# Four transposed loads a chunk instead of sixteen, and half the pause between a chunk's last load and its logits, in a convolution and mixture-of-experts kernel

## The chip, the cores and the metric

The kernel runs on one core of a Trainium2 chip. The metric is the device time of one execution in microseconds. The engines are TensorE (PE, matmuls; PEld its weight loads), VectorE (DVE), ScalarE (ACT), GpSimd (POOL) and SyncE (SP), which issues most of the DMAs.

## The reference

Eight sequences of 3,584 tokens with 192 features pass a causal convolution of 7 taps whose softmaxed weights differ by head; its 28,672 output tokens pass a mixture of 8 experts, one expert a token.

```python
# convolution: 8 heads of 24 features, softmax over the 7 taps
out = np.einsum('hk,bskhg->bshg', w, x_unf)          # (8, 3584, 192)
# routing and experts, x is out as (28672, 192)
xn = x / (norm(x) + 1e-6);  en = emb / (norm(emb) + 1e-6)
logits = xn @ en.T / tau
expert_idx = argmax(logits, axis=1)
probs = softmax(logits)                              # gate = probs[expert_idx]
for e in range(8):
    mask = expert_idx == e
    h = np.maximum(x[mask] @ w1[e], 0.0)             # (n, 1024)
    out[mask] = gate_w[mask, None] * (h @ w2[e])     # (n, 192)
```

## The kernel before

The tokens are cut into 16 chunks of 1,792: 16 tiles of 112 tokens (`TP`), token on the partition. A chunk passes these stages.

- `mix`: for each head one band matmul (L389) convolves all 16 tiles; ACT copies the result out (L392); ACT or DVE sums the squares.
- `route`: in four groups of four tiles (`GX`), `scaled` (L436, L438) and `rest` (L445 on) write each token as fp16 high and low parts into its row in `rows2`. A row has `RW` = 240 words of 4 bytes: 448 fp16 values, then the token's number and gate. `turn` (L624) transposes the rows' first 384 columns, so that features lie on the partitions: one DMA on SP's queue for each tile, written to a slot of `xtb`. After the last of them the stage pauses by `TURN`; then `logits` (L612) does three small matmuls a tile, and `rank` takes the argmax, the gate and each token's place (`pc`, `di`). Chunks 0 and 1 are transposed on TensorE, in the head; chunks 2 to 15 by these DMAs.
- `put`, `scatter` (L628): POOL writes each tile's rows by indirect DMA into `rows_d` in DRAM, sorted by expert.
- `hand_out`, after chunks 2, 3, 5, 8 and 12 (`PICK`), and `last_blocks` at the end: `select` (L663 to L712), some 20 tiny DVE instructions on one partition, chooses the expert and first row of blocks of 1,024, 512, 256 and at the end 128 tokens (`sel`). At the end nine scatters of zero rows (`pads`) come first.
- An expert block: `fetch` on SP reads the first row from `sel` (L745), loads the block's rows transposed (`e_xT`, two DMAs, L753) and the tokens' numbers and gates (`e_mt`, L757). For each of 8 steps five matmuls give the hidden values in PSUM (`h_ps`, L799), ACT takes the relu (L803), DVE the low part (L805). Then for each 128 tokens 24 matmuls (`o_ps`, L822), ACT scales them by the gate into `y` (L827, a ring of four buffers), and POOL writes them out by token number (`out_dram`, L829). Five PSUM banks serve `h_ps` and `o_ps` in turn.

The order is made when the kernel is built. The expert steps carry a clock (about 1.07 us for a step of first products and 1.92 for 128 tokens of second ones); a dispatcher puts the pieces of `mix` and `route` between them, and a pause such as `TURN` holds the next piece until the clock has moved on by that much. DMAs on SP stand in its program in the order in which they were written, and SP takes them one after another; a scheduler orders the other engines.

Of the kernel before, what the change touches and what calls it, by code (L numbers as in the profile page):

```python
# [12 lines left out]
F16 = mybir.dt.float16  # L13
# [12 lines left out]
D = 192  # L26
E = 8
# [4 lines left out]
CT = TP * NT  # L32
XD = 224
RW = 240


W2 = 3 * F
# [5 lines left out]
NFC = F // 128  # L43
PICK = (2, 3, 5, 8, 12)
GX = 4
XW = GX * 3 * TP
NACT = 3
PRE = 39
TURN, RANK, GAP = 14.0, 10.0, 0.5
STEP = 5 * 512 / 2400, 24 * D / 2400  # L50
RAW = 2 * (2 * F + F * D // 128)
AREAS = (1, 0), (1, 2), (1, 1), (0, 0), (0, 1), (1, 0), (0, 0), (0, 1)
# [23 lines left out]
class _Moe:  # L76
    def __init__(self, ctx, tc, x, weight, emb, tau, w1, w2, out):
        self.tc, self.nc = tc, tc.nc
        self.x, self.weight, self.emb, self.tau = x, weight, emb, tau
        self.w1, self.w2, self.out = w1, w2, out  # L80
        B, S, _ = x.shape
        self.B, self.S, self.N = B, S, B * S
        self.nch = self.N // CT
        self.per_b = S // CT
        self.cap = self.N + PAD
        self.dummy = E * self.cap
        pool = lambda name, bufs, **k: ctx.enter_context(
            tc.tile_pool(name=name, bufs=bufs, **k))
        self.cp = pool("const", 1)
        self.xp = pool("xload", 2)  # L90
        self.sp = pool("small", 2)
        self.lp = pool("lone", 1)
        self.ep = pool("expert", 3)
        self.yp = pool("y", 3)
        self.op = pool("out", 4)
        self.mp = pool("meta", 6)
        self.rings = {k: pool("ps_" + k, n, space=PSUM)
                      for k, n in (("r", 2), ("l", 1), ("h", 5))}

        self.res = self.cp.tile([128, E * RES], F16, name="res")  # L100
        self.work = self.cp.tile([128, 2 * NFC * 512 + S2 + RES - W2], F16, name="work")
        self.hid = self.work[:, 0:2 * NFC * 512]
        self.slot = self.work[:, 2 * NFC * 512:]
        self.xtb = self.cp.tile([128, NT // GX, XW + HALO], F16, name="xtb")
        self.rows2 = self.cp.tile([TP, 2, NT, RW], I32, name="rows2")
        self.ids = self.cp.tile([TP, NT], I32, name="ids")
        self.xtn = 0
        self.wexp = self.cp.tile([128, E, 2], I32, name="wexp")
        self.dp = pool("scratch", 1, space=DRAM)
        self.rows_d = self.dp.tile([E * self.cap + PAD, RW], I32, name="rows_d")  # L110
        self.scatters, self.pend, self.step = [], [], None
        self.nput, self.final = 0, False
        self.counts, self.pace = {}, 1.0
        self.xts, self.mixed = [], {}
        self.subs, self.ready, self.at, self.copied = [], 0, 0, 0
        self.clock, self.mm = 0.0, None
# [50 lines left out]

    def constants(self):
        nc, cp = self.nc, self.cp
        nc.gpsimd.memset(self.xtb[:, :, XW:], 0.0)  # L170
        nc.gpsimd.memset(self.rows2[:, :, :, XD + 2:], 0)
        nc.gpsimd.iota(self.ids, pattern=[[TP, NT]], base=TP - 1,
                       channel_multiplier=-1)
        head = self.ep.tile([128, 4 * 512], F16, tag="xT", name="head")[:].bitcast(F32)
        self.idf, self.onef = head[:, 0:128], head[:, 128:256]
        make_identity(nc, self.idf)
        self.idh = cp.tile([128, 128], F16, name="idh")
        nc.vector.tensor_copy(out=self.idh, in_=self.idf)
        nc.gpsimd.memset(self.onef, 1.0)
        self.oneh = cp.tile([128, 128], F16, name="oneh")  # L180
        nc.gpsimd.memset(self.oneh, 1.0)

        self.lth = cp.tile([128, 128], F16, name="lth")
        nc.gpsimd.memset(self.lth, 1.0)
        nc.gpsimd.affine_select(
            out=self.lth, in_=self.lth, pattern=[[1, 128]], base=0,
            channel_multiplier=-1, compare_op=ALU.is_gt, fill=0.0)

        tmp = self.op.tile([128, D], F32, tag="y", name="tmp")[:, 0:2 * E + 64].bitcast(I32)
        e8i = tmp[0:TP, 0:E]  # L190
        nc.gpsimd.iota(e8i, pattern=[[-1, E]], base=E, channel_multiplier=0)
        self.e8 = cp.tile([TP, E], F32, name="e8")
        nc.vector.tensor_copy(out=self.e8, in_=e8i)

        self.rst = cp.tile([TP, E, NT], F32, name="rst")
        nc.gpsimd.memset(self.rst, 1.0)
        nc.gpsimd.memset(self.rst[:, :, 0:1], 0.0)

        nums = tmp[0:1, E:E + 64]
        nc.gpsimd.iota(nums, pattern=[[1, 64]], base=0, channel_multiplier=0)  # L200
        self.nums = cp.tile([1, 64], F32, name="nums")
        nc.vector.tensor_copy(out=self.nums, in_=nums)

        cbi = tmp[:, E + 64:]
        nc.gpsimd.iota(cbi, pattern=[[self.cap, E]], base=0, channel_multiplier=0)
        self.cb = cp.tile([128, E], F32, name="cb")
        nc.vector.tensor_copy(out=self.cb, in_=cbi)

        self.start = cp.tile([1, E], F32, name="start")
        nc.vector.tensor_copy(out=self.start, in_=cbi[0:1, :])  # L210
# [231 lines left out]
    def rest(self, c, g):  # L442
# [5 lines left out]
        self.nc.vector.tensor_tensor(  # L448
            out=rows[:, u, 320:384], in0=xc[:, u, 128:192],
            in1=rows[:, u, 256:320], op=ALU.subtract)  # L450
        self.nc.vector.tensor_copy(out=rows[:, u, 384:448], in_=rows[:, u, 256:320])


    def route(self, c):
# [23 lines left out]
    def first(self, c):  # L478
# [9 lines left out]
        for v in steps:  # L488
# [4 lines left out]
            else:  # L493
# [4 lines left out]
                for a in range(GX):  # L498
# [2 lines left out]
                        in_=rows[:, g * GX + a, k * 128:(k + 1) * 128],  # L501
                        identity=self.idh[:TP, :TP])
                nc.scalar.copy(  # L503
                    out=xT[:, 0:XW].rearrange("p (a k t) -> p a k t", k=3, t=TP)[:, :, k, :],
                    in_=tp)
                if k == 2:
                    if g == 0:
# [6 lines left out]
    def rank(self, c, lg, f):  # L514
# [63 lines left out]
        di = sp.tile([TP, NT], I32, tag="di", name="di")  # L578
        nc.vector.tensor_single_scalar(out=di, in_=dr, scalar=-1.0, op=ALU.add)
        yield 0.8, 0.0  # L580
        self.pend += [(c, di[:, t:t + 1], r32[:, t, :]) for t in range(NT)]
        self.left += CT
        if c + 1 in PICK[1:]:
            self.hand_out(c + 1)
# [23 lines left out]
    def logits(self, lg, xT, g):  # L608
        for a in range(GX):
            for k in range(3):  # L610
                u = (a * 3 + k) * TP
                i = self.nc.tensor.matmul(  # L612
                    out=lg[:, g * GX + a, :], lhsT=xT[:, u:u + 128],
                    rhs=self.mb if k == 2 else self.ma,
                    start=(k == 0), stop=(k == 2))
                if k == 0:
                    self.behind(i)


    def turn(self, c, g):  # L620
        xT, rows, t = self.xt_next(), self.rows2[:, c % 2].bitcast(F16), g * GX
        xv = xT[:, 0:XW].rearrange("p (a k t) -> p a k t", k=3, t=TP)
        for a in range(GX):
            self.nc.sync.dma_start_transpose(out=xv[:, a], in_=rows[:, t + a, 0:2 * D])  # L624
        return xT

    def scatter(self, idx, src):
# [29 lines left out]
    def select(self, n, k, last, name, cb):  # L657
# [17 lines left out]
        nc.vector.scalar_tensor_tensor(out=bs, in0=ap, scalar=-float(n),  # L675
                                       in1=self.start, op0=ALU.mult, op1=ALU.add)
        jf = self.nums[:, 0:k]
        ge, df = one("ge", (1, k, E + 1), F16), one("df", (1, k, E))
        nc.vector.memset(ge, 1.0)
        nc.vector.tensor_tensor(  # L680
            out=ge[:, :, 1:], in0=a[:].unsqueeze(1).to_broadcast([1, k, E]),
# [3 lines left out]
        nc.vector.tensor_tensor(  # L685
            out=df, in0=df, in1=bs[:].unsqueeze(1).to_broadcast([1, k, E]),
            op=ALU.mult)
        ro, tm, se = one("ro", (1, k)), one("tm", (1, k)), one("se", (1, k))
        nc.vector.tensor_reduce(out=ro, in_=df, op=ALU.add, axis=AX.X)
        nc.vector.scalar_tensor_tensor(out=ro, in0=jf, scalar=float(n), in1=ro,  # L690
                                       op0=ALU.mult, op1=ALU.add)
# [353 lines left out]
```

## Time and profile before

| | us |
|---|---|
| three runs | 1232.15, 1233.92, 1236.98 |
| median | 1233.92 |
| the profiled execution | 1238.18 |
| its span | 1236.5 |
| TensorE busy | 1127.5 (91%) |
| DVE / ACT / POOL busy | 756.1 / 587.4 / 550.4 |

The span lies 1.7 us inside the profiled execution's time, and that execution 4.3 us above the median. A page of the profile gives the busy time of each engine, the span in 40 slices (about 31 us each), and groups of instructions by their line. In its last columns "<-" names what ended the idle time ahead of an instruction. The head, in which weights are loaded and chunks 0 and 1 are routed, takes until about 113 us; from there to about 842 us routing runs between expert blocks; after that there are expert blocks alone.

### The profile page before, as it was taken

To read this page: it belongs to the slowest core of one execution; us is meant where nothing else is said; L and a number is where in the kernel's file an instruction comes from. 1 tells how busy PE (TensorE), PEld (TensorE's weight loads), DVE (VectorE), ACT (ScalarE), POOL (GpSimd) and SP (SyncE) were. 2 spreads that over 40 slices of the span, in tenths; PEclk is the share of its full clock that TensorE was granted. 3 is DMA by queue.
4 is the path that set the end of the run, shared out by engine and by line. 5 is a ranking of instruction groups with operands and counts; after the bars stand their busy time and mean duration, and the time that the engine had idled before them with its cause. 6 is when DMAs were issued, how large, how long until landed. Compare 5 with 4: busy or idle time off the path is not lost.

```text
span 1236.5 us, 31375 instructions
## 1 busy us (share of the span) xinstructions
PE 1127.5 (91%) x10428; PEld 872.4 (71%) x10428; DVE 756.1 (61%) x2029; ACT 587.4 (48%) x1350; POOL 550.4 (45%) x522
## 2 busy tenths in 40 slices
PE   4675769899999899998989999999999999999998
PEld 2553658786677876756877676666677777898897
DVE  2899766886668757666675746553434453466365
ACT  4986445554554555563635454423333333333333
POOL 0074165574575645565745546673222222222222
PEclk9676879899999999999989999999999999999999
DMA  9945566576675576755638545326122231123121
GB/s 243 231 131 157 119 157 150 126 164 122 150 173 146 109 158 134 161 144 107 164 73 191 110 86 134 90 87 107 43 54 49 52 72 49 44 48 71 43 57 43
DMA packets 305818, 140.68 MB, mean 114 GB/s; under 512 B 247630, under 2 KB 296141, under 8 KB 305664
## 3 DMA queue, kind: packets, MB, share of 16 engines
q1 hardware_dynamic: 282000, 87.97, 34.3%
q0 software_dynamic: 23664, 50.68, 14.5%
q8 instruction: 94, 1.54, 0.5%
q14 instruction: 60, 0.49, 0.1%
HBM read 38.35 MB, written 51.05 MB: 72 GB/s over the span
## 4 chain that ended last, share of the span: by engine, by line
PE 37%; issue 8%; POOL 3%; DMA 3%; ACT 1%; DVE 1%; POOLq 0%; ACTq 0%; DVEq 0%
PE h_ps L799 18%; PE o_ps L822 17%; POOL out_dram L829 2%; POOL rows_d L628 1%; PE conv_ps L389 1%; DMA rows_d<-rows,di 1%; DMA xtb<-rows 1%; DMA out_dram<-y,e_mt 1%; ACT work L803 1%; DVE work L805 0%; DMA rows_d<-xtb,padi 0%; ACT rows L438 0%; ACT sq L402 0%; PE lg_ps L612 0%; DVE work L735 0%
## 5 line engine op out<-in xcount | busy, mean ns | idle before, releaser
L822 PE MATMUL o_ps<-work 128*128 128x192 f16 x5472 | 497.8, 248 | 21.3 <-DVE work L805 9.9
L822 PEld LDWEIGHTS <-work 128*128 128x128 f16 x5472 | 458.5, 99 | 59.9 <-DVE work L805 15.9
L829 POOL DMA_INDIRECT out_dram<-y,e_mt x228 | 255.1, 1119 | 470.8 <-ACT y L827 434.0
L805 DVE SCALAR_TENSOR_TENSOR work<-h_ps,work 128x512 f16<-128x512 f32 x456 | 311.1, 687 | 169.0 <-ACT work L803 165.2
L803 ACT ACTIVATE work<-h_ps 128x512 f16<-128x512 f32 x456 | 267.5, 596 | 236.5 <-PE h_ps L799 205.5
L628 POOL DMA_INDIRECT rows_d<-rows,di x256 | 281.6, 1100 | 141.4 <-issue 56.8
L799 PE MATMUL h_ps<-e_xT,res 128*128 128x512 f16 x1360 | 312.3, 382 | 6.9 <-DVE work L805 3.5
L799 PEld LDWEIGHTS <-res 128*128 x1360 | 131.8, 98 | 162.0 <-issue 19.7
L799 PE MATMUL h_ps<-e_xT,work 128*128 128x256 f16 (+1 forms) x2200 | 226.7, 259 | 15.2 <-DMA e_xT<-rows_d 10.2
L799 PEld LDWEIGHTS <-work 128*128 128x128 f16 x2200 | 187.4, 99 | 41.5 <-DMA e_xT<-rows_d 10.4
L827 ACT ACTIVATE y<-o_ps,g 128x192 f32<-128x192 f32 x228 | 92.8, 418 | 236.2 <-PE o_ps L822 209.7
L735 DVE COPY work<-res 128x3074 f16 x85 | 82.3, 968 | 165.2 <-PE o_ps L822 161.2
L389 PE MATMUL conv_ps<-xt,band 128*112 128x384 f32 x256 | 110.8, 534 | 14.9 <-ACT xt L392 8.0
L438 ACT CAST rows<-xt 112x768 f16<-112x768 f32 x64 | 53.0, 832 | 97.3 <-DMA rows_d<-rows,di 44.5
L392 ACT COPY xt<-conv_ps 112x384 f32<-112x384 f32 x128 | 60.3, 479 | 43.7 <-PE conv_ps L389 41.2
L402 ACT ACTIVATE sq<-xt 112x192 bf16<-112x192 f32 x204 | 73.6, 361 | 4.8
L445 DVE TENSOR_TENSOR rows<-xt,rows 112x512 f16<-112x512 f32 x64 | 44.2, 690 | 45.0 <-ACT rows L438 42.5
L389 PEld LDWEIGHTS conv_ps<-xt,band 128*112 128x112 f32 x256 | 42.7, 193 | 33.3 <-issue 14.5
L436 DVE TENSOR_TENSOR xt<-xt,x_p_s 112x768 f32<-112x768 f32 x64 | 58.6, 953 | 0.0
L732 DVE COPY work<-res 128x3072 f16 x56 | 53.7, 960 | 0.2 <-PE h_ps L799 0.2
L612 PEld LDWEIGHTS <-xtb 128*128 128x128 f16 x768 | 30.2, 98 | 26.7 <-DMA xtb<-rows 13.2
L612 PE MATMUL lg_ps<-ma,xtb 128*128 128x16 f16 x512 | 31.0, 171 | 14.3 <-ACT xtb L503 7.5
(158 smaller groups left out, 524.7 us busy)
## 6 DMA issues: line engine op xcount, KB each, us to landing
xt<-in_dram SPq DMA_DIRECT2D x8, 1536.0 KB
xt<-in_dram SPq DMA_DIRECT2D x7, 1440.0 KB
rows_d<-rows,di POOLq DMA_INDIRECT x256
out_dram<-y,e_mt POOLq DMA_INDIRECT x228
xtb<-rows SPq DMA_TRANSPOSE x224
res<-in_dram SPq DMA_DIRECT2D x4, 768.0 KB
work<-in_dram SPq DMA_DIRECT2D x4, 768.0 KB
e_xT<-rows_d SPq DMA_TRANSPOSE x184
```

The costliest lines, as they stand in the source:

```text
L389: self.behind(nc.tensor.matmul(out=ps, lhsT=self.band[:, h, :], rhs=xt[:, :, h * G:(h + 1) * G], start=True, stop=True))
L392: nc.scalar.copy(out=xc[:, :, h * G:(h + 1) * G], in_=ps)
L402: nc.scalar.activation(out=sq, in_=xc[:, t, :], func=AF.Square, accum_out=n2[:, t:t + 1])
L612: i = self.nc.tensor.matmul(out=lg[:, g * GX + a, :], lhsT=xT[:, u:u + 128], rhs=self.mb if k == 2 else self.ma, start=(k == 0), stop=(k = ...
L628: i = self.nc.gpsimd.indirect_dma_start(out=self.rows_d[:, :], out_offset=bass.IndirectOffsetOnAxis(ap=idx, axis=0), in_=src, in_offset=No ...
L735: self.nc.vector.tensor_copy(out=self.slot[:, S2:], in_=self.res[:, bass.ds(self.we + W2, RES - W2)])
L799: mm = nc.tensor.matmul(out=ps[:, c, :], lhsT=w1(o, b + c), rhs=xT[:, k, :], start=(i == 0), stop=(i == 4))
L803: self.step = nc.scalar.activation(out=hh[:, b:b + m, :], in_=ps, func=AF.Relu).ins
L805: nc.vector.scalar_tensor_tensor(out=hl[:, b:b + m, :], in0=ps, scalar=0.0, in1=hh[:, b:b + m, :], op0=ALU.max, op1=ALU.subtract)
L822: mm = nc.tensor.matmul(out=o, lhsT=h[:, c, q], rhs=w2[:, c, k:k + D], start=(c + i == 0), stop=(c == NFC - 1 and i == 2))
L827: self.step = nc.scalar.activation(out=y, in_=o, func=AF.Copy, scale=g[:, a:a + 1]).ins
L829: i = nc.gpsimd.indirect_dma_start(out=self.out[:, :], out_offset=bass.IndirectOffsetOnAxis(ap=mt[:, a, 0:1], axis=0), in_=y, in_offset=No ...
```

## The change

One DMA now transposes a group of four tiles. For this a row in `rows2` gets 256 words (`SW`), so that four rows of a token's partition are 2,048 fp16 columns in one piece: 16 blocks of 128, four a tile. The fourth block of each tile holds the row's remaining columns and isn't read by the logits; a slot of `xtb` has room for it. A scatter still writes 240 words. `TURN` goes from 14 to 7. Since `xtb` and `rows2` are larger, two of `select`'s tiles (`ge`, `df`) with three that lie inside the first (`ro`, `tm`, `se`) are now taken from the ring of the four `y` buffers, and the scratch for the descriptors of POOL's DMAs is halved.

```diff
+SW = 256
-XW = GX * 3 * TP
+XW = GX * 4 * TP
-TURN, RANK, GAP = 14.0, 10.0, 0.5
+TURN, RANK, GAP = 7.0, 10.0, 0.5
...
-        self.xtb = self.cp.tile([128, NT // GX, XW + HALO], F16, name="xtb")
-        self.rows2 = self.cp.tile([TP, 2, NT, RW], I32, name="rows2")
+        self.xtb = self.cp.tile([128, NT // GX, XW], F16, name="xtb")
+        self.rows2 = self.cp.tile([TP, 2, NT, SW], I32, name="rows2")
...
-        nc.gpsimd.memset(self.xtb[:, :, XW:], 0.0)
+        nc.gpsimd.memset(self.xtb[:].rearrange(
+            "p h (a k t) -> p (h a) k t", k=4, t=TP)[:, :, 3, 0:HALO], 0.0)
...
-        self.nc.vector.tensor_copy(out=rows[:, u, 384:448], in_=rows[:, u, 256:320])
+        self.nc.vector.tensor_copy(out=rows[:, u, 384:452], in_=rows[:, u, 256:324])
...
-        self.pend += [(c, di[:, t:t + 1], r32[:, t, :]) for t in range(NT)]
+        self.pend += [(c, di[:, t:t + 1], r32[:, t, 0:RW]) for t in range(NT)]
...
-                u = (a * 3 + k) * TP
+                u = (a * 4 + k) * TP
...
-        xv = xT[:, 0:XW].rearrange("p (a k t) -> p a k t", k=3, t=TP)
-        for a in range(GX):
-            self.nc.sync.dma_start_transpose(out=xv[:, a], in_=rows[:, t + a, 0:2 * D])
+        self.nc.sync.dma_start_transpose(
+            out=xT.rearrange("p (n t) -> p n t", t=TP),
+            in_=rows[:, t:t + GX, :].rearrange("p a c -> p (a c)"))
...
-        ge, df = one("ge", (1, k, E + 1), F16), one("df", (1, k, E))
+        tmp = self.op.tile([128, D], F32, tag="y", name="sl_ge")[0:1]
+        ro, tm, se = (tmp[:, i * k:(i + 1) * k] for i in (5, 6, 7))
+        ge = tmp.bitcast(F16)[:, 0:k * (E + 1)].rearrange("p (k e) -> p k e", e=E + 1)
+        df = self.op.tile([128, D], F32, tag="y", name="sl_df")[0:1, 0:k * E].rearrange(
+            "p (k e) -> p k e", e=E)
...
-        ro, tm, se = one("ro", (1, k)), one("tm", (1, k)), one("se", (1, k))
...
-                    dynamic_dma_scratch_size=8192)
+                    dynamic_dma_scratch_size=4096)
```

The order on the engines moves with it. The first place is SP's queue around the transposed loads of chunk 4 (`xtb<-rows_91`), between the fetches of expert blocks; ISA rows are register work of a fetch. Before:

```order
L745 TENSOR_LOAD sel_3584_1718
L745 ISA x2
L753 ISA
L753 DMA_TRANSPOSE e_xT<-rows_d 128x3x256
L753 ISA
L753 DMA_TRANSPOSE e_xT<-rows_d 128x1x256
L757 ISA
L757 DMA e_mt<-rows_d 128x2x2
L624 DMA_TRANSPOSE xtb<-rows_91 128x3x112 x8
L364 DMA xt<-in_dram 112x192
L373 DMA xt<-in_dram 128x15x192
L624 DMA_TRANSPOSE xtb<-rows_91 128x3x112 x8
```

and of the changed kernel:

```order
L762 ISA
L762 DMA e_mt<-rows_d 128x2x2
L624 DMA_TRANSPOSE xtb<-rows_91 128x16x112 x2
L366 DMA xt<-in_dram 112x192
L375 DMA xt<-in_dram 128x15x192
L624 DMA_TRANSPOSE xtb<-rows_91 128x16x112 x2
L750 TENSOR_LOAD sel_3584_1574
L750 ISA x2
L758 ISA
L758 DMA_TRANSPOSE e_xT<-rows_d 128x3x256
L758 ISA
L758 DMA_TRANSPOSE e_xT<-rows_d 128x1x256
```

Four loads stand for sixteen, and the first fetch of the selection's blocks (the TENSOR_LOAD of `sel_3584` at the top of the piece before), which stood ahead of the loads, now stands behind the last of them.

The second place is DVE at the first of the four selections of the end, between residuals of an expert block (L805, L810 now); `[waits ...]` names the semaphores that an instruction waits for, DMASW those of POOL's DMAs. Before:

```order
L805 SCALAR_TENSOR_TENSOR work<-h_ps,work 128x512 [waits Activation_49]
L672 SCALAR_TENSOR_TENSOR sl_a<-rst,sl_av 1x8 [waits DVE_49]
L674 TENSOR_TENSOR sl_ap<-sl_a,sl_av 1x8 [waits DVE_49]
L680 TENSOR_TENSOR sl_ge<-sl_a,nums 1x3x8
L805 SCALAR_TENSOR_TENSOR work<-h_ps,work 128x512 [waits Activation_49]
L675 SCALAR_TENSOR_TENSOR sl_bs<-sl_ap,start 1x8 [waits DVE_49]
L708 TENSOR_SCALAR sl_t<-sl_ap 1x8
L683 TENSOR_TENSOR sl_df<-sl_ge 1x24 [waits DVE_49]
L700 TENSOR_REDUCE sl_se<-sl_ge 1x3
L710 TENSOR_SCALAR sl_t<-sl_t 1x8 [waits DVE_49]
L685 TENSOR_TENSOR sl_df<-sl_df,sl_bs 1x24 [waits DVE_49]
```

and of the changed kernel:

```order
L740 COPY work<-res 128x3074 [waits PE_49]
L819 TENSOR_SCALAR g<-e_mt,work 128x4 [waits DMAHW5_49,DVE_49]
L810 SCALAR_TENSOR_TENSOR work<-h_ps,work 128x512 [waits Activation_49] x8
L685 MEMSET sl_ge 1x27 [waits DMASW3_49,DMASW5_49,DMASW2_49,DMASW0_49]
L686 TENSOR_TENSOR sl_ge<-sl_a,nums 1x3x8 [waits DVE_49]
L705 TENSOR_REDUCE sl_ge<-sl_ge 1x3 [waits DVE_49]
L674 SCALAR_TENSOR_TENSOR sl_a<-rst,sl_av 1x8
L706 TENSOR_SCALAR sl_ge<-sl_ge 1x3 [waits DVE_49]
L676 TENSOR_TENSOR sl_ap<-sl_a,sl_av 1x8 [waits DVE_49]
L709 CAST sel_11008_12306<-sl_ge 1x3 [waits DVE_49]
```

The selection's first write to `sl_ge` (L680 before; the memset L685 now, since the tile isn't set ahead any more) has moved behind the next block's weight copy (L740), gates (L819) and eight residuals, and it waits for four of POOL's DMAs, the writes of earlier `y` buffers.

The third place is POOL from the `pads` on (`rows_d<-xtb,padi`), with the scatters of the last chunks (`rows_d<-rows_91,di`) and the outputs of the block then running. Before:

```order
L829 DMA out_dram<-y,e_mt 28672x192 x4
L628 DMA rows_d<-xtb,padi 230528x240 x9
L628 DMA rows_d<-rows_91,di 230528x240 x10
L829 DMA out_dram<-y,e_mt 28672x192
L628 DMA rows_d<-rows_91,di 230528x240
L829 DMA out_dram<-y,e_mt 28672x192
L628 DMA rows_d<-rows_91,di 230528x240
```

and of the changed kernel:

```order
L834 DMA out_dram<-y,e_mt 28672x192 x4
L630 DMA rows_d<-xtb,padi 230528x240 x9
L630 DMA rows_d<-rows_91,di 230528x240 x12
L834 DMA out_dram<-y,e_mt 28672x192
L630 DMA rows_d<-rows_91,di 230528x240
L834 DMA out_dram<-y,e_mt 28672x192
L630 DMA rows_d<-rows_91,di 230528x240
```

The first output behind the pads has moved from behind ten scatters to behind twelve.

## Rows read from the trace of the kernel before

**Rows 1.** The page: busy time, clock slices, and two groups by line

```profile
PE 1127.5 (91%) x10428; PEld 872.4 (71%) x10428; DVE 756.1 (61%) x2029; ACT 587.4 (48%) x1350; POOL 550.4 (45%) x522
...
PEclk9676879899999999999989999999999999999999
...
L389 PE MATMUL conv_ps<-xt,band 128*112 128x384 f32 x256 | 110.8, 534 | 14.9 <-ACT xt L392 8.0
...
L445 DVE TENSOR_TENSOR rows<-xt,rows 112x512 f16<-112x512 f32 x64 | 44.2, 690 | 45.0 <-ACT rows L438 42.5
```

**Rows 2.** Waits of TensorE, 120 to 850 us: total, times, longest

```profile
PE lg_ps L612 <- DMA xtb<-rows: 11.7, 9, 3.7
PE h_ps L799 <- DMA e_xT<-rows_d: 10.2, 2, 6.0
...
PE h_ps L799 <- ACT y L827: 5.1, 2, 4.3
```

**Rows 3.** Timeline of TensorE: start, duration, work, [idle before <- releaser]

```profile
127.09 0.21 PE L612 MATMUL lg_ps<-ma,xtb 128*128 128x16 f16 x2 [3.67 <-DMA xtb<-rows]
...
173.67 0.22 PE L612 MATMUL lg_ps<-ma,xtb 128*128 128x16 f16 x2 [3.08 <-DMA xtb<-rows]
...
181.51 4.87 PE L799 MATMUL h_ps<-e_xT,work 128*128 128x256 f16 x22 [6.02 <-DMA e_xT<-rows_d]
```

**Rows 4.** Timeline of the queue of SP, 100 to 300 us

```profile
124.73 10.27 SPq L624 DMA_TRANSPOSE xtb<-rows  x8
...
165.39 12.24 SPq L624 DMA_TRANSPOSE xtb<-rows  x8
178.41 2.53 SPq L753 DMA_TRANSPOSE e_xT<-rows_d  x2
...
208.26 0.46 SPq L364 DMA_DIRECT2D xt<-in_dram  x1
...
209.24 14.72 SPq L624 DMA_TRANSPOSE xtb<-rows  x8
```

**Rows 5.** Stretches: length, busy by engine, PEclk, DMA share, GB/s

```profile
861.50:864.50 3.00, 3.00 (x39) 3.00 (x38) 0.20 (x1) 0.54 (x2) 0.25 (x1) 1.00 1.26 178
128.60:135.40 6.80, 5.74 (x43) 5.43 (x43) 4.01 (x11) 0.00 (x0) 0.00 (x0) 0.50 0.36 76
173.00:186.70 13.70, 6.18 (x48) 4.41 (x49) 5.26 (x18) 2.26 (x4) 10.69 (x10) 0.50 0.76 163
227.60:234.40 6.80, 5.46 (x37) 3.98 (x38) 4.28 (x13) 2.03 (x3) 4.61 (x5) 0.50 0.54 122
323.20:326.60 3.40, 3.40 (x9) 1.13 (x8) 3.40 (x10) 1.57 (x3) 2.02 (x2) 0.50 0.72 146
```

**Rows 6.** Timeline of TensorE around the last block selection, 805 to 842 us

```profile
810.93 6.91 PE L799 MATMUL h_ps<-e_xT,res 128*128 128x512 f16 x30
...
822.62 8.09 PE L822 MATMUL o_ps<-work 128*128 128x192 f16 x96 [1.22 <-ACT work L803]
...
835.85 1.24 PE L799 MATMUL h_ps<-e_xT,res 128*128 128x512 f16 x5 [0.82 <-ACT y L827]
```

**Rows 7.** Lines L624 and L753: SP's transposed loads, ns min/median/max

```profile
L624 SPq DMA_TRANSPOSE xtb<-rows x224: 1174/1252/4145, 124.7 to 766.7; - x112
...
L753 SPq DMA_TRANSPOSE e_xT<-rows_d x184: 1130/1236/2622, 113.0 to 1229.9; - x184
```

**Rows 8.** Timeline of POOL: first pad, and first output of the block

```profile
800.41 0.96 POOL L628 DMA_INDIRECT rows_d<-xtb,padi  x1 [4.08 <-issue]
...
824.95 0.99 POOL L829 DMA_INDIRECT out_dram<-y,e_mt  x1 [0.30 <-issue]
```

**Rows 9.** Timeline of ACT: an output that waits for its buffer

```profile
827.42 0.42 ACT L827 ACTIVATE y<-o_ps,g 128x192 f32<-128x192 f32 x1 [5.38 <-DMA out_dram<-y,e_mt]
```

**Rows 10.** Timeline of DVE: first instruction of the second and third selection

```profile
804.58 0.14 DVE L663 TENSOR_TENSOR sl_av<-cb,start 1x8 f32<-1x8 f32 x1
...
808.39 0.15 DVE L663 TENSOR_TENSOR sl_av<-cb,start 1x8 f32<-1x8 f32 x1
```

More of the change, by code (lines that the diff above doesn't have):

```diff
@@ L503, in first @@
                 nc.scalar.copy(
-                    out=xT[:, 0:XW].rearrange("p (a k t) -> p a k t", k=3, t=TP)[:, :, k, :],
+                    out=xT[:, 0:XW].rearrange("p (a k t) -> p a k t", k=4, t=TP)[:, :, k, :],
                     in_=tp)
```

## The prediction

> **What bounds the kernel now.** I read the page first: TensorE is busy for 1127.5 of the 1236.5 us, and its clock slices are mostly at 9 behind the head [rows 1]. So the kernel can gain only from the 109 us in which TensorE stands still, and from stretches at half clock. Next come the waits of TensorE between 120 and 850 us, where routing runs beside the expert blocks: 11.7 us in nine waits of the logits for a transposed load into xtb, 10.2 us in two waits of the first expert product for its fetched rows e_xT, and 5.1 us in two waits whose releaser is ACT's y [rows 2]. TensorE's own timeline gives the long ones: 3.67 us at 127.09 and 3.08 at 173.67 (xtb), and 6.02 at 181.51 (e_xT) [rows 3], which leaves 4.2 for the other e_xT wait. The queue of SP explains the e_xT ones. Eight transposed loads of xtb stand in it from 165.39 for 12.24 us, and the fetch that ends the wait at 181.51 is issued behind them, at 178.41; eight more from 209.24 hold it for 14.72 us, until 223.96 [rows 4]. Last come the clock stretches: TensorE was granted 0.50, its 1.2 GHz level, in 173.0–186.7 and 227.6–234.4, around the two e_xT waits, and in 128.6–135.4 and 323.2–326.6, behind xtb waits [rows 5]. What half clock costs is in the rows too: 22 matmuls of 256 columns took 4.87 us there, 221 ns each [rows 3], where 30 of 512 columns took 6.91, 230 ns each [rows 6].
>
> **Part 1, the loads on SP.** Fourteen chunks times sixteen loads become four loads each: 56 for 224. One small load holds SP for 1.25 us at the median, and one e_xT load for 1.24, although half of these carry three blocks of 128 columns and half carry one [rows 7]. So the hold doesn't grow with the data in this trace, and I take 1.25 for the large one: 5 us a chunk, where a half chunk now takes 12.24 to 14.72 [rows 4]. Its upper bound is a hold that grows with the data: 16 blocks for 3, 1.25 × 16/3 = 6.7 us, 26.7 a chunk, about what is there now. The data itself: 112 partitions × 4,096 B = 458,752 B a load, a third more than four small ones, for the fourth block of each tile is loaded and never used. The nearest row moves an e_xT load of 512 tokens at 178 GB/s [rows 5] (its first row): 2.6 us a load, 10.3 a chunk, beside TensorE's work. The lower bound is the hold, 1.25; the upper one again 6.7. I take 2.6.
>
> What goes first are the two e_xT waits. With SP's loads done after 5 us and not 25, and with one or two fetches now issued behind the xtb loads where they stood ahead of them, the fetch still gets its place some 10 us earlier than at 178.41. Of 10.2 us I leave 1: **−9.2**. The bounds are 0 (the data of the large loads holds the same queue, and the fetch waits behind that) and −10.2. With them goes the half clock that follows them: 6.18 us of work at half clock in 173.0–186.7 and 5.46 in 227.6–234.4 [rows 5] would take half: 3.1 + 2.7 = **−5.8**. The stretches behind the xtb waits I leave as they are.
>
> The Trainium skill ("DMA: Bandwidth & Descriptors", section "Latency and other measured facts") gives a DMA transpose 261 GB/s where the middle dimension isn't contiguous. By it a load would take an estimated 1.76 us and a chunk 7.0, not 10.3; the row's 178 GB/s is lower, and no run here shows yet which of them holds for the large load. By the page's figure the xtb term below would be nearer its lower bound.
>
> **Part 2, the pause.** Half the pause brings a chunk's logits nearer to its last rows. For chunk 8, TensorE's program has between the last rows and the logits of the third group 92 matmuls of 192 columns, 40 of 256 and 2 of the convolution; before, 192, 122 and 8. At 84 ns (96 in 8.09 us) and 115 ns (half of 230) [rows 6] and 534 ns [rows 1] that is 7.7 + 4.6 + 1.1 = 13.4 us, for 16.1 + 14.0 + 4.3 = 34.4 before. By the same count chunk 2 has 10.9, chunks 3 to 5 have 13 to 18. What has to fit in there: the last rows' DVE copies, 0.69 us each [rows 1] with residuals between them, about 3; two x loads on SP, 0.9 (the loads of 208.26 stand just ahead of 209.24); then the load: from issue to its use a small one took 2.36 us (124.73 [rows 4] to 127.09 [rows 3]), a large one 1.3 more by the two data times (2.6 for 1.25), and one large load ahead of it in the queue 2.6 more. In all 10 to 11 us for the third group, 13 for the fourth. So the margin is thin: in most chunks there is none to lose, in two or three it just fails. Per wait the new stall is 1 to 4 us, as 3.08 and 3.67 now. I take 6 us over the chunks, for 11.7 now: **−5.7**. Bounds: 0 left (−11.7), and 1 to 2 us in each of 14 chunks, about 21 (+9).
>
> **Part 3, the tiles of the block selection.** Two tiles of each selection now come out of the ring of four y buffers, so a selection can begin on DVE only when the y that stood there has been written out by POOL. The four mid selections (after chunks 3, 5, 8, 12) now have such waits, but the y's there are mostly long out: 2 us in all, **+2**, bounds 0 and 4 × 8.
>
> At the last one the wait is sure. POOL starts nine pads and ten scatters at 800.41, and the first out of the block then running comes at 824.95 [rows 8], so one scatter takes 1.29; the next order puts two more scatters ahead, so that out moves from 24.5 to 27.1 us after the pads' start. It needs 2.47 us to free its y: ACT's y at 827.42 waited for it, after 5.38 us [rows 9]. So the first selection's first tile is free at 29.5 after the pads' start, its second at 32. DVE has done the eight residuals ahead of it by 21 or 22 (their products begin at 810.93 [rows 6] and take about 11 us), and all behind the first selection wait: the other selections and the next block's residuals. A selection alone takes 3.8 us (804.58 to 808.39) [rows 10]: the first ends at 33.5, the third near 41, the fourth by 44. TensorE still has its 96 second products, 22.2 to 30.3 on that scale (822.62 − 800.41, 8.09 long) [rows 6]; the next block's first products find one PSUM bank free of five, since the y's that would empty the others need buffers that the selections hold. So TensorE stands from about 31.5 to 41 or 43, 9 to 11 us. Before, it lost 4.4 there: 1.22 at 822.62, 0.82 at 835.85, and 2.4 in three waits between them and beside them [rows 6] (two of the five). So +6, and a half-clock stretch of the size behind the 6.02 us wait, 3.1 for 1.7 at present (a stretch of 3.4 us at half clock): **+7.5** in all. Bounds: 0 (if the products ahead reach further than I count) and +12.
>
> **The small edits.** The halo's memset lies in the head, where other engines carry the span; the last rows' copy goes from 64 to 68 columns, 6% of a part of 0.69 us, four times a chunk. Half the descriptor scratch for POOL's DMAs isn't seen in the trace: zero if eight still fit (each already waits for the one eight back); if each had to wait for its forerunner to land, 2.4 for 1.29 us a scatter, and routing would lag. I take 0: no row shows POOL waiting on its ring now.
>
> **Sum.** On the profiled run's own 1238.2: −9.2 − 5.8 − 5.7 + 2 + 7.5 = −11.2, so 1227.0. The median of the runs shown is 4.3 lower (1233.9), so **1222.7, say 1223**, 0.9% faster.
>
> **Rivals.** (1) *The selections are hidden:* +7.5 and +2 fall to about 0, by TensorE having more to do than I count. For it: before, waits of that place are only 4.4. Against: all y's need POOL, which is full there. Time 1213. (2) *The pause takes back what the queue gives:* xtb waits stay at 11.7 or grow somewhat, because the logits come 20 us earlier against loads that carry a third more. For it: the margins above, 10.9 and 13.4 for 10 to 13 needed. Then −9.2 − 5.8 + 2 + 7.5 = −5.5, and half-clock stretches behind new xtb waits take 3 of them: about 1232. This is the case of no measurable change. (3) *Slower, by the selections:* at all five hand-outs DVE stops for y's whose outs are queued on POOL behind scatters. Price about 8 us each, 40 in all for a gain of 20.7: 1233.9 + 19 = 1253. It decides if POOL's queue at the mid hand-outs is more than some six DMAs behind (6 × 1.29 = 8). For it: POOL is full in 173.0–186.7, 10.69 of 13.70 us [rows 5]. Against: outside the last hand-out, [rows 2] has 5.1 us in only two waits that y releases. (4) *Slower, by the hold:* a large load holds SP for 6.7 us; the queue is as full as before, nothing comes of part 1, and logits that come 20 us earlier lack 2 to 6 us a chunk: 1233.9 + 9.5 + 14 × 2 = 1271 at the low end. Against it [rows 7]. Should the change not do what it says (the scheduler puts the gained time back elsewhere), it is case 2.
>
> **Numbers.** A measurement of this kernel can tell about 0.5% from no change, so faster is below 1227.7 and slower above 1240.1. Forecast 45%, with 1215 to 1229 as its own range; hidden selections 13%; pause takes it back 26%; slower by selections 11%, by the hold 5%. Of the forecast's 45, 5 lie above 1227.7 and count as same; of the 26, 2 are slower; of the two slower cases' 16, 4 come out smaller than priced and count as same. Faster 0.40 + 0.13 = 0.53, same 0.05 + 0.24 + 0.04 = 0.33, slower 0.02 + 0.12 = 0.14. The range goes from 1210, under the second case, to 1240, above the no-change case.
>
> **What would show it.** SP's rows of the transposed load: four a chunk near 1.25 us each (6 or more: case 4). The waits of the first expert product for e_xT: about 1 us, and granted clock 1.00 around 181 and 228 us, where it is 0.50 now. The logits' waits for xtb: near 6; 12 or more is case 2. DVE's memset at a selection, and what ended the wait before it: about 8 us idle at the last, released by out_dram; such waits at four hand-outs too make case 3. TensorE's gap near the last selection: 9 to 11 us. I'd be wrong by my largest term if the e_xT waits stayed with SP's queue empty.

## The result, and the profile after

Fifteen runs of each kernel gave a median of 1243.48 us (1234.66 to 1249.55) after the change and 1236.98 us (1230.71 to 1240.21) before. The ratio is 1.0056, interval 1.0034 to 1.0077: the kernel became slower by half a per cent, where 0.9% faster was forecast, and the time lies above the range. The profiled execution of the changed kernel has a span of 1239.8 us, 3.3 more than before.

The page of the changed kernel, busy times and the granted clock in 40 slices:

```profile
PE 1128.7 (91%) x10428; PEld 870.7 (70%) x10428; DVE 757.9 (61%) x2029; ACT 587.4 (47%) x1350; POOL 547.2 (44%) x522
...
PEclk9666889899999999999999999989999999999999
```

TensorE is busy for 1128.7 us where it was 1127.5 [rows 1], so the work is the same, and two thirds of the 3.3 us are idle time. Its waits between 120 and 850 us (total, times, longest):

```profile
PE h_ps L804 <- DVE work L810: 15.0, 9, 8.8
PE o_ps L827 <- DVE work L810: 10.6, 17, 3.0
PE h_ps L804 <- ACT y L832: 9.9, 2, 5.1
PE lg_ps L614 <- DMA xtb<-rows: 7.5, 4, 3.7
...
PE conv_ps L391 <- issue: 4.9, 1, 4.9
```

Against [rows 2] the two waits for e_xT, 10.2 us, are gone; xtb is down from 11.7 to 7.5. In their place stand waits for DVE's residuals (L810), of which one alone is 8.8 us, and waits for ACT's y, 9.9 for 5.1. The queue of SP shows why the fetches are in time:

```profile
175.01 2.52 SPq L758 DMA_TRANSPOSE e_xT<-rows_d  x2
...
179.01 7.28 SPq L624 DMA_TRANSPOSE xtb<-rows  x2
...
193.54 10.38 SPq L624 DMA_TRANSPOSE xtb<-rows  x2
205.18 2.52 SPq L758 DMA_TRANSPOSE e_xT<-rows_d  x2
...
226.56 4.43 SPq L624 DMA_TRANSPOSE xtb<-rows  x2
...
236.65 10.69 SPq L624 DMA_TRANSPOSE xtb<-rows  x2
```

A half chunk of transposed loads (eight before, two now) took 10.27 to 14.72 us [rows 4]; in these rows it takes 4.43 to 10.69. That isn't the 2.5 us of the prediction, since one large load holds SP for longer than a small one (ns, min/median/max):

```profile
L624 SPq DMA_TRANSPOSE xtb<-rows x56: 1419/2890/8316, 123.0 to 754.1; - x56
```

The median is 2.89 us for 1.25 [rows 7]. Then the last selections. POOL, from the first pad on, with the first outputs of the block then running:

```profile
794.79 0.96 POOL L630 DMA_INDIRECT rows_d<-xtb,padi  x1 [1.77 <-issue]
...
821.67 0.99 POOL L834 DMA_INDIRECT out_dram<-y,e_mt  x1 [0.31 <-issue]
...
824.22 0.99 POOL L834 DMA_INDIRECT out_dram<-y,e_mt  x1 [0.30 <-DMA out_dram<-y,e_mt]
```

DVE, the last residual ahead of the selection, and the first writes to the selection's two tiles:

```profile
817.09 0.69 DVE L810 SCALAR_TENSOR_TENSOR work<-h_ps,work 128x512 f16<-128x512 f32 x1 [0.39 <-ACT work L808]
824.24 0.08 DVE L685 MEMSET sl_ge<- 1x27 f16 x1 [6.46 <-DMA out_dram<-y,e_mt]
...
826.66 0.17 DVE L689 TENSOR_TENSOR sl_df<-sl_ge 1x24 f32<-1x24 f16 x1 [0.76 <-DMA out_dram<-y,e_mt]
```

TensorE at the same place:

```profile
816.26 8.08 PE L827 MATMUL o_ps<-work 128*128 128x192 f16 x96
824.18 1.24 PE L804 MATMUL h_ps<-e_xT,res 128*128 128x512 f16 x5
834.22 2.29 PE L804 MATMUL h_ps<-e_xT,res 128*128 128x512 f16 x5 [8.80 <-DVE work L810]
838.07 5.27 PE L804 MATMUL h_ps<-e_xT,res 128*128 128x512 f16 x15 [1.56 <-DVE sl_ap L676]
```

The first output goes out 26.9 us after the first pad, the memset runs 29.45 us after it and the first write to sl_df 31.9: the prediction had 27.1, 29.5 and 32. TensorE has finished its 96 second products and five more, and stands for 8.80 us and again for 1.56. The clock falls with it: over these 13.6 us the mean granted clock is 0.55, near the lower level of 0.50 (length, busy by engine, PEclk, DMA share, GB/s):

```profile
829.60:843.20 13.60, 7.42 (x20) 2.54 (x20) 9.74 (x52) 3.15 (x7) 6.16 (x6) 0.55 0.64 121
```

### The profile page after: what moved, and what is told of

It reads as the page before. It is cut to its first block, busy times and chain, and to the rows that moved or that the text cites. A ratio compares the mean times of both kernels' runs of the same rounds, so it can differ in the third digit from the quotient of the medians.

```text
span 1239.8 us, 31094 instructions
## 1 busy us (share of the span) xinstructions
PE 1128.7 (91%) x10428; PEld 870.7 (70%) x10428; DVE 757.9 (61%) x2029; ACT 587.4 (47%) x1350; POOL 547.2 (44%) x522
## 3 DMA queue, kind: packets, MB, share of 16 engines
q0 software_dynamic: 23664, 50.68, 13.9%
## 5 line engine op out<-in xcount | busy, mean ns | idle before, releaser
L827 PE MATMUL o_ps<-work 128*128 128x192 f16 x5472 | 490.6, 247 | 22.2 <-DVE work L810 12.0
L834 POOL DMA_INDIRECT out_dram<-y,e_mt x228 | 249.8, 1096 | 443.7 <-ACT y L832 387.4
L810 DVE SCALAR_TENSOR_TENSOR work<-h_ps,work 128x512 f16<-128x512 f32 x456 | 312.5, 687 | 167.2 <-ACT work L808 161.8
L804 PE MATMUL h_ps<-e_xT,res 128*128 128x512 f16 x1360 | 313.2, 381 | 13.4 <-DVE work L810 11.5
L804 PE MATMUL h_ps<-e_xT,work 128*128 128x256 f16 (+1 forms) x2200 | 230.4, 260 | 13.4 <-ACT y L832 9.9
L740 DVE COPY work<-res 128x3074 f16 x85 | 82.3, 969 | 194.4 <-PE o_ps L827 193.8
L391 PE MATMUL conv_ps<-xt,band 128*112 128x384 f32 x256 | 114.8, 550 | 16.4 <-ACT xt L394 5.0
L391 PEld LDWEIGHTS conv_ps<-xt,band 128*112 128x112 f32 x256 | 43.5, 198 | 33.7 <-issue 16.4
```

The costliest lines, as they stand in the source:

```text
L391: self.behind(nc.tensor.matmul(out=ps, lhsT=self.band[:, h, :], rhs=xt[:, :, h * G:(h + 1) * G], start=True, stop=True))
L740: self.nc.vector.tensor_copy(out=self.slot[:, S2:], in_=self.res[:, bass.ds(self.we + W2, RES - W2)])
L804: mm = nc.tensor.matmul(out=ps[:, c, :], lhsT=w1(o, b + c), rhs=xT[:, k, :], start=(i == 0), stop=(i == 4))
L810: nc.vector.scalar_tensor_tensor(out=hl[:, b:b + m, :], in0=ps, scalar=0.0, in1=hh[:, b:b + m, :], op0=ALU.max, op1=ALU.subtract)
L827: mm = nc.tensor.matmul(out=o, lhsT=h[:, c, q], rhs=w2[:, c, k:k + D], start=(c + i == 0), stop=(c == NFC - 1 and i == 2))
L834: i = nc.gpsimd.indirect_dma_start(out=self.out[:, :], out_offset=bass.IndirectOffsetOnAxis(ap=mt[:, a, 0:1], axis=0), in_=y, in_offset=No ...
```

## The experiments

Ratios are to the kernel before, run on the same chip beside it; times are medians. "Own tiles" means that the selection's five tiles have buffers of their own again; to make room for them the descriptor scratch is 2048.

### First: which part costs

`a_own`: the changed kernel with own tiles.

```diff
-        tmp = self.op.tile([128, D], F32, tag="y", name="sl_ge")[0:1]
-        ro, tm, se = (tmp[:, i * k:(i + 1) * k] for i in (5, 6, 7))
-        ge = tmp.bitcast(F16)[:, 0:k * (E + 1)].rearrange("p (k e) -> p k e", e=E + 1)
-        df = self.op.tile([128, D], F32, tag="y", name="sl_df")[0:1, 0:k * E].rearrange(
-            "p (k e) -> p k e", e=E)
+        ge, df = one("ge", (1, k, E + 1), F16), one("df", (1, k, E))
...
+        ro, tm, se = one("ro", (1, k)), one("tm", (1, k)), one("se", (1, k))
...
-                    dynamic_dma_scratch_size=4096)
+                    dynamic_dma_scratch_size=2048)
```

> The changed kernel with the selection's five tiles back in buffers of their own (to make room, the descriptor scratch is 2048 instead of 4096). Theory A (the loss is the wait of the last selection for y buffers, 8.8 + 1.6 us idle on TensorE for 4.4 before, and 1.6 more by half clock, 7.6 in all): the ratio to the kernel before falls from 1.0056 to about 0.9995 (1236 us), and no gap over 3 us stands behind the last of the 96 second products. Theory B (the halved pause and the larger loads cost time in the middle, the selection is covered elsewhere): ratio stays at 1.004 or more. Theory C (the smaller descriptor scratch holds POOL back): ratio at or above 1.0056.

Measured: 1227.78 us, ratio 0.9907 (0.9884 to 0.9929). That is more than theory A had: the tiles in the ring cost 1.0056/0.9907, 1.5% or some 18 us (the two ratios come from different chips, each against the kernel before on its own), and loads and pause without them gain 11.5 us. TensorE of this kernel around the last selections:

```profile
811.41 8.09 PE L824 MATMUL o_ps<-work 128*128 128x192 f16 x96 [1.06 <-ACT work L805]
819.34 4.48 PE L801 MATMUL h_ps<-e_xT,res 128*128 128x512 f16 x20
825.09 1.36 PE L801 MATMUL h_ps<-e_xT,res 128*128 128x512 f16 x5 [1.27 <-ACT y L829]
827.83 6.37 PE L801 MATMUL h_ps<-e_xT,res 128*128 128x512 f16 x15 [1.38 <-DVE work L807]
```

The gaps are 1.06, 1.27 and 1.38 us, of the size of those before the change [rows 6]; the 8.80 is gone.

`b_ring`: the kernel before with only these tiles in the ring (the same edit the other way round).

> The kernel before with only the selection's tiles moved into the ring of y buffers. Theory A: slower by 6 to 8 us, ratio 1.005 to 1.0065, with a gap of 8 to 10 us on TensorE at the last selections, released by DVE behind out_dram. Theory B or C: ratio within 0.999 to 1.002.

Measured: 1252.08 us, ratio 1.0109 (1.009 to 1.0129), some 13 us by this edit alone. DVE's first write to the selection's tile, and TensorE behind it:

```profile
831.60 0.08 DVE L683 MEMSET sl_ge<- 1x27 f16 x1 [5.91 <-DMA out_dram<-y,e_mt]
```

```profile
841.64 2.29 PE L802 MATMUL h_ps<-e_xT,res 128*128 128x512 f16 x5 [8.30 <-DVE work L808]
```

The mechanism of the last selection is there, with 8.30 us of gap, but the cost is larger than that place, and twice what was expected.

`b_scr2048`: the kernel before with a quarter of the scratch.

```diff
-                    dynamic_dma_scratch_size=8192)
+                    dynamic_dma_scratch_size=2048)
```

> The kernel before with only the descriptor scratch of POOL's DMAs cut from 8192 to 2048; the order on all engines is the same. Theory A: no change, ratio 0.999 to 1.001, scatters 1.25 us apart as before. Theory C: slower by 4 us or more, ratio 1.003 or above, and scatters further apart than 1.29 us.

Measured: 1240.29 us, ratio 1.0002 (0.9984 to 1.002). POOL's scatters (busy, mean ns | idle before them, releasers):

```profile
L628 POOL DMA_INDIRECT rows_d<-rows,di x256 | 281.2, 1098 | 142.3 <-issue 58.4 <-ACT work L803 43.5 <-DVE w_s L321 17.6
```

The mean is 1098 ns, as before (1100). Theory C is out, and `a_own` may be read without regard to its scratch.

`b_turn7`: the kernel before with the pause alone.

```diff
-TURN, RANK, GAP = 14.0, 10.0, 0.5
+TURN, RANK, GAP = 7.0, 10.0, 0.5
```

> The kernel before with only the pause halved (TURN 7), sixteen loads a chunk. Theory A (the pause by itself costs, since the queue holds 20 to 25 us of loads for a chunk; the larger loads pay for it): slower, waits of the logits for xtb of 30 us or more for 11.7, ratio 1.01 to 1.03. Theory B (the pause is what hurts in the changed kernel too): the same sign, and a_own stays above 1.004. If the pause is free: ratio 0.998 to 1.002 and xtb waits near 12 us.

Measured: 1235.65 us, ratio 0.9973 (0.9954 to 0.9992). Its waits on TensorE for loads:

```profile
PE lg_ps L612 <- DMA xtb<-rows: 21.4, 22, 3.7
...
PE h_ps L799 <- DMA e_xT<-rows_d: 2.7, 1, 2.7
```

The xtb waits nearly double, from 11.7 to 21.4 us, but the e_xT waits fall from 10.2 to 2.7, so the two together hardly change. None of the expectations had the small gain, and these rows don't explain it.

### Second: where the ring costs, and what loads and pause do apart

`a_lastring` and `a_midring`: `a_own` with the ring in the four selections of the end only (`self.final`), and in those ahead of them only (`not self.final`).

```diff
+        ring = self.final
+        if ring:
+            tmp = self.op.tile([128, D], F32, tag="y", name="sl_ge")[0:1]
...
+        else:
+            ge, df = one("ge", (1, k, E + 1), F16), one("df", (1, k, E))
...
```

> Selection tiles of their own up to chunk 12, from the ring of y buffers only in the four selections of the end (scratch 2048). The whole ring cost a_own to changed kernel is 1.0056 / 0.9907, about 18 us. Theory A2 (some 5 to 8 us of it at the end, the rest at the mid hand-outs and in the order that they bring): ratio to the kernel before 0.995 to 0.998, gap of 8 to 10 us on TensorE behind DVE at the end. Theory D (all of it at the end): 1.004 to 1.006.

> The other half: the ring for the selections after chunks 2 to 12, own tiles for the four at the end (scratch 2048). Theory A2: ratio 0.997 to 1.001, the middle like that of the changed kernel, no gap over 3 us at the end. Theory D: 0.990 to 0.992, like a_own.

Measured: `a_lastring` 1233.13 us, 0.9973 (0.9955 to 0.999); `a_midring` 1238.73 us, 1.001 (0.9993 to 1.0028). Against `a_own` (measured on another chip) the end costs 0.66%, 8 us, and the middle 1.03%, 12.7 us; the two add up to somewhat more than the 18 us of both, within the intervals. Theory D is out; the larger half of the loss is in the middle.

`a_own_turn14` and `a_own_turn4`: `a_own` with the old pause, so large loads alone, and with a still shorter one (TURN 14 and 4 for 7).

> Large loads alone: own selection tiles and the old pause (TURN 14), scratch 2048. If loads and pause add (the pause alone gave 0.9973): 0.9907 / 0.9973, ratio 0.992 to 0.995. If the large loads pay only with the short pause: 0.997 to 1.001. If the loads do it all and the pause nothing: 0.990 to 0.992. In each case the waits of the first expert product for e_xT should be under 3 us (10.2 before).

> Own selection tiles, large loads, pause 4 for 7, scratch 2048. If there is margin left behind the large loads: ratio 0.987 to 0.991. If the pause of 7 is at the edge (third group's data late): xtb waits of 20 us or more for 4.5 in a_own, ratio 0.994 to 1.002.

Measured: 1233.19 us, 0.9973 (0.9955 to 0.9991), and 1231.95 us, 0.9967 (0.9947 to 0.9987). Loads alone gain 0.27%, the pause alone gained 0.27%, both 0.93%: together more than the sum of the two, so `a_own_turn14` falls into the case that large loads pay mainly with the short pause. Waits for e_xT with the large loads alone were 3.9 us, so the expectation of under 3 missed. With a pause of 4 xtb waits were 6.9 us, not the 20 of the pessimistic side, yet the time is 0.6% above that of pause 7; I have no row for that difference.

### Third: lack of buffers, or the order

`after_y6`: the changed kernel with six y buffers (and scratch 2048). `a_own_margin`: `a_own` with `MARGIN` 44 for 22, by which the scatters of a chunk stand earlier between the expert steps. `a_own_turn8`, `after_turn8`: `a_own` and the changed kernel with a pause of 8.

```diff
-        self.op = pool("out", 4)
+        self.op = pool("out", 6)
...
-MARGIN = 22
+MARGIN = 44
...
-TURN, RANK, GAP = 7.0, 10.0, 0.5
+TURN, RANK, GAP = 8.0, 10.0, 0.5
```

> The changed kernel with six y buffers for four (scratch 2048); selection tiles still from that ring. Theory A2 (too few y buffers for outputs and selection together): the tile that a selection gets is one whose output went out longer ago; ratio to the kernel before 0.991 to 0.998, the 6.5 us wait of DVE for out_dram at the first of the last selections under 1 us or moved to a later one. Theory E (the buffers aren't the cause, the order that the scheduler then makes is): ratio 1.002 to 1.007.

> Own selection tiles, large loads, pause 7, and the scatters of a chunk's rows placed earlier between the expert steps (MARGIN 44 for 22). Theory F (behind the shorter queue the next limit is that ACT's write of a chunk's rows waits for the scatters of two chunks before, 72.5 us of ACT's waits in a_own for 44.5 before): these waits fall to under 50 us and the ratio is 0.985 to 0.989. Rival: POOL is then late with the outputs, the waits of ACT's y for out_dram grow from 18 us, ratio 0.992 to 1.000.

> a_own with a pause of 8 for 7, as a measure of how much any new order moves the time. If a_own's 0.9907 is a property of the pause near 7: 0.989 to 0.993. If it was one order among many with a spread of half a per cent: 0.993 to 0.999, between a_own and the 0.9973 of pause 14.

> The changed kernel with a pause of 8 for 7. Beside a_own_turn8 it measures the cost of the ring once more in other orders. Theory A2 (ring costs 8 us at the end and more in the middle): 1.0 to 1.5% above a_own_turn8, ratio 1.002 to 1.010. Theory E (the middle part of it is an accident of the order): 0.5 to 0.8% above a_own_turn8.

On the chip of these four runs the kernel before took 1331.65 us, and it and the three kernels that were run elsewhere too took 7 to 9% longer than there. In `a_own_turn8` TensorE stands idle for long where the profile shows no releaser:

```profile
PE o_ps L824 <- issue: 39.2, 45, 5.4
```

Ratios were 1.0105 (1.0057 to 1.0154), 1.0149 (1.0096 to 1.0202), 0.9989 (0.9956 to 1.0022) and 1.0048 (1.0016 to 1.0079). With stalls of that size they tell little. Three of the kernels were measured on another chip as well (labels in _r), with `a_own_y5` (five y buffers for four in `a_own`) as a control.

> The changed kernel with six y buffers for four (scratch 2048), on another chip. Lack of buffers: ratio 0.991 to 0.998, the wait of DVE at the first of the last selections (6.5 us) shorter or moved to a later selection, the middle (to 780 us) 5 us or more shorter than in the changed kernel. Order: 1.002 to 1.007, the middle as in the changed kernel.

> Own selection tiles, large loads, pause 7, and five y buffers for four, as control. If y buffers are short even without the selections (5.6 us of waits for y in a_own): ratio 0.984 to 0.989. If four do there: 0.989 to 0.994, as a_own.

> a_own with a pause of 8 for 7, on another chip. One lucky order at 7: 0.993 to 0.999. A property of pauses near 7: 0.989 to 0.993.

> The changed kernel with a pause of 8 for 7, on another chip. If the ring costs some 18 us in any order: 1.2 to 1.8% above a_own_turn8_r. If the middle part is an accident of one order: 0.5 to 0.9% above it.

Measured: `after_y6_r` 1237.33 us, 0.9987 (0.9968 to 1.0006); `a_own_y5` 1227.27 us, 0.9899 (0.9874 to 0.9923); `a_own_turn8_r` 1227.18 us, 0.9894 (0.9868 to 0.992); `after_turn8_r` 1235.07 us, 0.9964 (0.9945 to 0.9982). So `a_own` wasn't lucky in the one order of pause 7, a fifth buffer by itself does nothing, and the ring costs 0.7% at pause 8 for 1.5% at pause 7. By the expectation of `after_turn8_r` that 0.7% is the sign of the rival, a cost in the middle that is an accident of one order, and `after_y6_r` lies between its two cases. Where each of them pays is seen when the second products are counted in TensorE's records. The table has the time at which the 3,072nd and the 3,264th of 5,472 end, shortly ahead of the last selections and behind them:

| kernel | tiles: middle, end | 3,072nd | 3,264th | between |
|---|---|---|---|---|
| before | own, own | 807.1 | 847.7 | 40.6 |
| `b_ring` | ring, ring | 811.7 | 859.0 | 47.3 |
| `a_own` | own, own | 796.1 | 838.2 | 42.1 |
| `a_own_turn8_r` | own, own | 796.1 | 837.6 | 41.5 |
| `a_own_y5` | own, own | 797.4 | 836.9 | 39.5 |
| `a_own_turn14` | own, own | 801.6 | 842.2 | 40.6 |
| `a_own_turn4` | own, own | 804.1 | 840.2 | 36.1 |
| `a_lastring` | own, ring | 798.9 | 845.8 | 46.9 |
| `a_midring` | ring, own | 807.7 | 849.0 | 41.3 |
| after | ring, ring | 803.8 | 851.0 | 47.2 |
| `after_turn8_r` | ring, ring | 807.5 | 847.8 | 40.3 |
| `after_y6_r` | ring, ring | 806.3 | 846.8 | 40.5 |

With large loads and a pause of 7 or 8 the middle ends at 796.1 to 798.9 in the four kernels with own tiles there and at 803.8 to 807.7 in the four with the ring, 9 us later on the mean and at both pauses; what is missing at pause 8 is the end. Six buffers don't change the middle, so a plain lack of buffers isn't its cause. But with own tiles and a pause of 14 or 4 it ends at 801.6 and 804.1: another order moves this point by up to 8 us as well. And with small loads the ring costs only 4.6 there (811.7 for 807.1). So the ring costs time in the middle at every pair compared, but how much of the 9 us would be left in other orders isn't shown. The end costs 5 to 7 us in three of the five kernels with the ring there. In `after_turn8_r` the selections stand where no output is waited for, and it costs nothing. With six buffers it costs nothing either: DVE still waits once at the end, but TensorE's gap shrinks. The waits of DVE (total, times, longest) and that gap of `after_y6_r`:

```profile
DVE sl_ge L685 <- DMA out_dram<-y,e_mt: 5.8, 1, 5.8
```

```profile
836.86 1.48 PE L804 MATMUL h_ps<-e_xT,res 128*128 128x512 f16 x5 [2.41 <-DVE work L810]
```

### Fourth: what took the gain of loads and pause

`a_own_margin33` and `a_own_margin11`: `a_own` with the scatters earlier (shown below) and, with 11 in place of 33, later.

```diff
-MARGIN = 22
+MARGIN = 33
```

> a_own with the scatters of a chunk's rows placed earlier between the expert steps (MARGIN 33 for 22). Theory F (the casts' wait for scatters is the next limit): that wait falls from 72.5 us to under 60, ratio to the kernel before 0.985 to 0.989 (a_own 0.9907). Rival (the wait is there, but TensorE doesn't hang on it, and earlier scatters hold up the outputs on POOL): ratio 0.990 or more.

> a_own with the scatters placed later (MARGIN 11 for 22). Theory F: the casts' wait for scatters grows to 85 us or more, ratio 0.993 to 1.000. Rival: ratio within 0.002 of a_own's 0.9907.

Measured: 1228.05 us, 0.9921 (0.9892 to 0.995), and 1243.08 us, 1.0041 (1.0024 to 1.0057). The waits of ACT's row casts for the scatters of two chunks before, between 120 and 850 us, in the kernel before:

```profile
ACT rows L438 <- DMA rows_d<-rows,di: 44.5, 13, 8.2
```

in `a_own`:

```profile
ACT rows L440 <- DMA rows_d<-rows,di: 72.5, 18, 8.2
```

with the scatters earlier (33):

```profile
ACT rows L440 <- DMA rows_d<-rows,di: 67.8, 16, 8.2
```

and with them later (11):

```profile
ACT rows L440 <- DMA rows_d<-rows,di: 110.8, 29, 8.7
```

Theory F holds on one side: with 38 us more of that wait the time is 1.3% longer, beyond the range that was expected. On the other side it failed: earlier scatters took 5 us off the wait, where over 12 were expected, and nothing off the time.

## Why the prediction was wrong

- **The e_xT waits (−9.2):** right, 10.2 us went to none. The reason was half right: a large load holds SP for 2.89 us, not 1.25, about what its data was estimated to take (2.6). The two chunks shown take 15 to 18 us of SP (4.43 + 10.69, 7.28 + 10.38), not the 5 that the term used, and not 25 as before. That a hold doesn't grow with the data was read from loads of one and of three blocks, and was wrong for one of 16. Nor is the shorter hold all of it: the pause alone, with the small loads, took these waits to 2.7 us (`b_turn7`), the loads alone to 3.9.
- **The half clock behind them (−5.8):** too much for the changed kernel. Summed over slices of 3.4 us between 119 and 782 us, busy time times what the clock lacked, TensorE lost 16.4 us before and 13.9 after: −2.5. For loads and pause themselves the size was right: in `a_own` the sum is 9.4, −7.0, and in the other three kernels with own tiles in the middle and a pause of 7 or 8 it is 10.3 to 11.5. With the ring it is 12.2 to 13.9, so the stalls that the ring brings took some 2 us of the term back.
- **The xtb waits (−5.7):** 11.7 to 7.5, −4.2, and to 4.5 in `a_own`. The thin margin that the count of the third group showed was there; it didn't break.
- **The last selections (+7.5):** right in place, mechanism and size. The times of the three steps agree within 0.3 us, the table gives 47.2 − 40.6 = 6.6 in the trace, and `a_lastring` 8 us.
- **The mid selections (+2):** this is the step that failed. It said that the y's there are mostly long out, and took 2 of a range of 0 to 32. `a_midring` measured 12.7 us, the table 9. It also counted four selections; the trace has seven at those four places, two tiles each. DVE's own waits for outputs are small there, as I had said: in all of the changed kernel those for `sl_ge` are the row below, of which 6.5 us belong to the last selections (`sl_df` adds 0.8 there).

```profile
DVE sl_ge L685 <- DMA out_dram<-y,e_mt: 10.6, 3, 6.5
```

  So the price isn't where the prediction (and its third rival, which priced the same wait at 8 us a hand-out) looked for it. What does differ is ACT's y. The selection's tiles take places in the ring among the y's, so some y's now wait for outputs; an example in the changed kernel:

```profile
172.21 0.42 ACT L832 ACTIVATE y<-o_ps,g 128x192 f32<-128x192 f32 x1 [6.97 <-DMA out_dram<-y,e_mt]
```

  TensorE stands 5.05 us behind it; at the same place of `a_own` ACT waits 8.11 us for a scatter, and TensorE stands 3.44. Over the middle it adds up: with large loads and a pause of 7 or 8, TensorE's waits for ACT's y between 120 and 850 us are 3.9 to 6.6 us in the four kernels with own tiles in the middle and 9.9 to 15.0 in the four with the ring, 8 us more on the mean. In `b_ring`, where the middle costs 4.6, they don't grow (4.3 for 5.1). So y's that wait for outputs are the likely price at large loads, but no run takes them away by themselves, and why six buffers leave them (12.7) stays open.
- **What took the place of the waits that went (no term):** the second step that failed. Of the 20.7 us that loads and pause promised, `a_own` shows 11.5. TensorE's waits in it, for 8.5, 3.5, 5.1 and 11.7 before in the same order ([rows 2] has the last two):

```profile
PE o_ps L824 <- DVE work L807: 15.7, 19, 2.8
PE h_ps L801 <- DVE work L807: 11.7, 6, 4.2
PE h_ps L801 <- ACT y L829: 5.6, 3, 3.9
PE lg_ps L614 <- DMA xtb<-rows: 4.5, 4, 2.3
```

  The three terms came in, and more: e_xT −10.2, half clock −7.0, xtb −7.2. But the waits for DVE's residuals have grown by 15.4 us, which leaves 9.0 of the 24.4; the span of the trace fell by 9.8. The sum had put nothing against the waits that went. Why residuals are waited for is open. The casts of rows on ACT now wait for scatters for 72.5 us in place of 44.5, and relus stand behind them on ACT. Yet in `a_own_margin11`, where the casts wait for 110.8 us, TensorE's waits for residuals are 20.3 us (10.5 + 9.8), fewer than the 27.4 here, so the casts aren't shown to be their cause.
- **The scratch (0):** right, 1.0002.

The sum then: −11.5 for −20.7, and about +18 for +9.5, which makes the 6.5 us by which the kernel is slower. Both errors went the same way. The two steps that failed are thus the price of the ring in the middle, and the waits put at nothing that followed those that went.

The best kernel found is `a_own` with pause 7 or 8: 0.9907 and 0.9894, about 1% faster than before; pauses 14 and 4 give a third of that. It is the change without its loan from the y buffers.

## What to carry to other kernels

A tile that moves into another's ring of buffers takes part in that ring's whole order: price it at every place where it is allocated, by the writers that must now wait, and not by its own wait alone. When a memory-saving edit rides along with a speed-up, time the speed-up without it first. And waits that go can uncover others: here 24 us of waits and half clock went, and 15 us of waits for DVE's residuals came.

## What the runs showed of the hardware

A transposed load of 458,752 bytes held SP's queue for 1.42 to 8.32 us, 2.89 at the median, where one of a sixteenth of a chunk held it for 1.25 at the median. The Trainium skill ("DMA: Bandwidth & Descriptors", "Latency and other measured facts") has 261 GB/s for a DMA transpose with a middle dimension that isn't contiguous, an estimated 1.76 us for this load; if the hold is the data's time, the median here is 159 GB/s, so the measurement is well below the page. The rows of this load lie in one piece, so that it may not even be of the kind that this figure is for. Cutting the descriptor scratch to a quarter changed POOL's scatters by 2 ns in 1,100 (`b_scr2048`). And one chip ran four kernels 7 to 9% slower than another did, in the one trace shown with 39 us of unexplained idle time in front of one group of matmuls alone.
